# Attention scores accumulated over a whole head in four PSUM banks, four matmuls to one weight load

## The chip, the cores and the metric

The kernel runs on one core of a Trainium2 chip. The metric is the device time of one execution in microseconds (us), lower is better; the time given for a kernel is the median of several executions.

## The reference

One decode step of a transformer layer: layer norm, attention of one query token over a cache of 65,536 keys and values, then a gated MLP.

```python
q = (layernorm(x) @ wq)                  # 32 query heads of 128
# 8 KV heads, 4 query heads share one: k_cache, v_cache are [8, 65536, 128] bf16
scores = einsum("bhqd,bhkd->bhqk", q, k) * 128 ** -0.5
o = softmax(scores) @ v                  # per head
h = x + o @ wo
out = h + (sigmoid(g) * u) @ w_down      # g, u = layernorm(h) @ w_gate, @ w_up
```

K and V together are 268 MB, read once. Everything else is small.

## The kernel before

A KV head's 65,536 keys are four *blocks* of 4 MB (one DMA each), and a block is eight *chunks*. A ring of four 4 MB slots takes K and V blocks in turn; all loads are issued from one queue in a fixed order, each as soon as the load that had its slot is used up. DVE transposes each chunk of K in 32x32 pieces from the ring into a small key buffer; PE multiplies it with the query (which sits as "weights" in the array) and accumulates in a PSUM bank.

```python
NKT = 6          # key buffers, one chunk each
NS = 5           # PSUM banks for scores, one block each
...
def freed(ld):   # what a slot's next load waits for
    return {"wq": "q", "K": f"T{b}.{NC - 1}", "V": f"PV{b}"}[k]
...
def dve_block(b):
    for c in range(NC):                       # 8 chunks
        deps = [f"K{b}"] if c == 0 else []
        if n >= NKT: deps.append(f"S{(n - NKT) // NC}.{(n - NKT) % NC}")
        op("dve", lambda e, d=dst, sr=src: e.transpose(d, sr), deps, f"T{b}.{c}")
    op("dve", lambda e: e.tensor_reduce(M_sb[...], ps(b % NS, 0, 512), AX.X, ALU.max), [f"S{b}"], f"mx{b}")

def pe_scores(b):
    for c in range(NC):
        for je in range(4):                   # the weights differ for every (c, je)
            op("pe", lambda e, ...: e.matmul(ps(b % NS, 0, 512), lhsT=w_ap(h, je, c), rhs=kt_ap(n, je),
                start=(c == 0 and je == 0), stop=(c == NC - 1 and je == 3)), ...)
...
for b in range(NB + 4):                       # program order on every engine
    if b < NB:
        dve_block(b); pe_scores(b)
        if b % NR == NR - 1: softmax(b // NR)
    v = b - NR
    if v >= 0:
        if v % NR == 0: denominators(v // NR)
        pv(v)                                 # 32 matmuls, each with its own weights
        if v % NR == NR - 1: head_out(v // NR)
        if v == NB - 4: project7()
# ... last projection and the MLP follow
```

The weights of chunk c are the head's queries shifted by c columns, so that the eight chunks of a block land in different rows of one bank. That is why a block needs 32 weight loads for 32 matmuls.

## Time and profile before

| | before |
|---|---|
| time, median of 3 (range) | 667.71 us (667.36 to 667.81) |
| span of the profiled execution | 665.9 us |
| bytes read from HBM | 282.33 MB |
| DMA busy / PE / DVE / weight loads | 98.9% / 60% / 54% / 24% |

The first extract is from the page of the profile. Its first line gives busy time, share of the span and number of instructions; in the DMA strip each digit is a fortieth of the span in tenths; `q1` are the kernel's loads and `q8` instruction fetches (packets, MB, share of all DMA engines' time); the line that starts with DMA 67% is the chain of waits by engine; the last four are groups of instructions: busy us, mean ns | idle time of the engine before them and what ended it.

```profile
PE 396.3 (60%) x2545; PEld 162.8 (24%) x2545; DVE 359.2 (54%) x408; ACT 34.1 (5%) x90; POOL 8.5 (1%) x12
...
DMA  9999999999999999999999999999999999999996
...
q1 hardware_dynamic: 11560, 282.33, 98.9%
q8 instruction: 20, 0.33, 0.2%
...
DMA 67%; DVE 22%; PE 9%; ACT 1%; issue 0%; SPq 0%
...
L356 PE MATMUL PS<-ktw 128*128 128x512 bf16 x1024 | 294.1, 449 | 201.3 <-DVE ktw L342 196.1
L342 DVE STREAM_TRANSPOSE ktw<-ring 128x1024 f32<-128x1024 f32 x256 | 292.1, 1207 | 180.9 <-DMA ring<-in_A_k_cache_dram 180.9
L356 PEld LDWEIGHTS PS<-ktw 128*128 128x128 bf16 x1024 | 107.4, 110 | 384.6 <-DVE ktw L342 243.7
...
L343 DVE TENSOR_REDUCE M_sb<-PS 128x1 f32<-128x512 f32 x32 | 22.1, 692 | 49.9 <-PE PS L356 49.9
```

The DMA strip is full in all slices but the last, at a rate (282.33 MB over 665.9 us, 424 GB/s) near what the loads ever reach. The Trainium skill, "DMA: Bandwidth & Descriptors", section "Where 436 GB/s comes from", gives 435 GB/s as the ceiling of the path; the trace agrees with 431 to 432 in the steady state. PE idles 201 us before its score matmuls, nearly always for DVE, and DVE idles 181 us for K to land. So PE waits for DVE and DVE waits for DMA.

The second is from the chain of waits in order of time: start us, us, what.

```profile
57.08 1.05 PE PS L356 x4
...
121.26 9.14 DVE ktw L342 x8
...
130.42 29.67 DMA ring<-in_A_k_cache_dram
...
160.11 9.14 DVE ktw L342 x8
...
633.59 24.59 DMA ring<-in_B_w_up_dram
```

Two K/V pairs (16.78 MB) pass in 160.11 - 121.26 = 38.85 us, which is 432 GB/s. The 9.14 us of DVE in each period look like critical time, because a K load is issued when the transposes two K blocks earlier are done. But the load then takes 29.67 us to land, where 4.19 MB alone need 9.7: other loads are still ahead of it in the queue. Note also the first line, `57.08 1.05`: from the end of a block's last transpose to the end of its last four matmuls.

### The profile page before, as it was taken

What the parts mean: (1) busy time and instruction counts of PE and PEld (TensorE: products, weight loads), DVE (VectorE), ACT (ScalarE), POOL (GpSimd) and SP (SyncE); (2) the same over time, 40 slices, a digit from 0 to 9 for tenths busy, and PEclk for the clock granted to TensorE, in tenths of its full rate; (3) what the DMA queues carried; (4) which work ended last, traced back from release to release, by engine and by line L of the source; (5) the groups of instructions that cost most, each with busy time, mean ns of one, the idle gap of its engine ahead of it and who ended that gap; (6) DMA issues with size and microseconds to landing.
All of it is one profiled execution on the core that took longest, in us unless ns stands there. A gap on an engine that the chain in (4) does not pass through costs nothing.

```text
span 665.9 us, 5728 instructions
## 1 busy us (share of the span) xinstructions
PE 396.3 (60%) x2545; PEld 162.8 (24%) x2545; DVE 359.2 (54%) x408; ACT 34.1 (5%) x90; POOL 8.5 (1%) x12
## 2 busy tenths in 40 slices
PE   3778586565458664555665644666554567655344
PEld 2522232222123221222222212222221222223212
DVE  6579865574447655464555744476544645553002
ACT  0200100020002000020000200010000200002000
POOL 4000000000000000000000000000000000000000
PEclk9789798677787866788876778887677987768566
DMA  9999999999999999999999999999999999999996
GB/s 378 440 433 417 439 436 425 428 439 428 423 440 433 423 435 433 430 427 438 429 427 436 430 430 429 432 433 429 435 425 436 429 426 439 430 429 409 427 426 249
DMA packets 11586, 282.70 MB, mean 425 GB/s; under 512 B 1193, under 2 KB 2218, under 8 KB 2602
## 3 DMA queue, kind: packets, MB, share of 16 engines
q1 hardware_dynamic: 11560, 282.33, 98.9%
q8 instruction: 20, 0.33, 0.2%
q14 instruction: 4, 0.03, 0.0%
q10 hardware_dynamic: 2, 0.00, 0.0%
HBM read 282.33 MB, written 0.00 MB: 424 GB/s over the span
## 4 chain that ended last, share of the span: by engine, by line
DMA 67%; DVE 22%; PE 9%; ACT 1%; issue 0%; SPq 0%
DMA ring<-in_A_k_cache_dram 58%; DVE ktw L342 21%; PE PS L356 6%; DMA ring<-in_A_v_cache_dram 4%; DMA ring<-in_B_w_up_dram 4%; DMA ring<-in_A_wq_dram 2%; PE PS L307 1%; PE PS L419 1%; DVE M_sb L343 1%; ACT ktw L324 0%; DVE PT_sb L388 0%; PE PS L521 0%; PE PS L497 0%; SPq L239 0%; DVE hh L513 0%
## 5 line engine op out<-in xcount | busy, mean ns | idle before, releaser
L356 PE MATMUL PS<-ktw 128*128 128x512 bf16 x1024 | 294.1, 449 | 201.3 <-DVE ktw L342 196.1
L342 DVE STREAM_TRANSPOSE ktw<-ring 128x1024 f32<-128x1024 f32 x256 | 292.1, 1207 | 180.9 <-DMA ring<-in_A_k_cache_dram 180.9
L356 PEld LDWEIGHTS PS<-ktw 128*128 128x128 bf16 x1024 | 107.4, 110 | 384.6 <-DVE ktw L342 243.7
L419 PE MATMUL PS<-ring,PT_sb 128*16 128x512 bf16 x1024 | 70.6, 424 | 21.1 <-DMA ring<-in_A_v_cache_dram 21.1
L343 DVE TENSOR_REDUCE M_sb<-PS 128x1 f32<-128x512 f32 x32 | 22.1, 692 | 49.9 <-PE PS L356 49.9
L419 PEld LDWEIGHTS PS<-ring,PT_sb 128*16 128x16 bf16 x1024 | 28.4, 113 | 53.8 <-DMA ring<-in_A_v_cache_dram 25.3
L376 ACT ACTIVATE negmax<-PS 128x1 f32<-128x1 f32 x8 | 1.4, 171 | 550.2 <-PE PS L374 550.2
L388 DVE STREAM_TRANSPOSE PT_sb<-P_sb 128x512 bf16<-128x512 bf16 x32 | 21.8, 711 | 11.9 <-ACT P_sb L385 11.9
L433 DVE CAST O<-PS 128x4 bf16<-128x4 f32 x8 | 1.3, 162 | 39.1 <-PE PS L430 39.1
L385 ACT ACTIVATE P_sb<-PS,negmax 128x512 bf16<-128x512 f32 x32 | 21.6, 685 | 0.3
L307 PE MATMUL PS<-ring,xz 128*32 128x128 bf16 x128 | 9.7, 253 | 3.0 <-DMA ring<-in_A_wq_dram 3.0
L307 PEld LDWEIGHTS PS<-ring,xz 128*32 128x32 bf16 x128 | 9.6, 116 | 3.0 <-issue 3.0
L284 POOL TENSOR_TENSOR rstd<-ve,nhalf 128x1 f32<-128x1 f32 x2 | 1.1, 554 | 645.6 <-DVE ve L282 645.6
L430 PE MATMUL PS<-sel_bf,po_sb 128*128 128x4 bf16 x32 | 2.0, 168 | 11.4 <-ACT po_sb L427 11.4
L427 ACT ACTIVATE po_sb<-PS,rl 128x512 bf16<-128x512 f32 x8 | 5.5, 693 | 45.1 <-PE PS L419 45.1
L367 PE MATMUL PS<-identf,gm 128*1 128x128 f32 x16 | 3.0, 271 | 7.8 <-DVE gm L365 7.8
L385 ACT ACTIVATION_READ_ACCUMULATOR P_sb<-PS,negmax 128x1 f32 x32 | 6.5, 202 | 0.0
L456 PE MATMUL PS<-O,ktw 128*128 128x1 bf16 x128 | 4.9, 173 | 2.6 <-DMA ktw<-in_A_wo_dram 2.4
L257 DVE TENSOR_SCALAR rows_i<-rows_i 128x128 int32<-128x128 int32 x1 | 6.1, 6101 | 0.0
L259 DVE TENSOR_SCALAR cols_i<-cols_i 128x128 int32<-128x128 int32 x1 | 6.0, 6028 | 0.0
L374 PE MATMUL PS<-one_f,gmrep 1*128 1x1 f32 x16 | 3.0, 256 | 4.9 <-DVE gmrep L371 4.9
L456 PEld LDWEIGHTS PS<-O,ktw 128*128 128x128 bf16 x128 | 4.6, 118 | 2.9 <-DMA ktw<-in_A_wo_dram 2.2
(72 smaller groups left out, 56.8 us busy)
## 6 DMA issues: line engine op xcount, KB each, us to landing
ring<-in_A_k_cache_dram SPq DMA_DIRECT2D x32, 4096.0 KB, 29.7
ring<-in_A_v_cache_dram SPq DMA_DIRECT2D x31, 4096.0 KB, 35.6
ring<-in_A_wq_dram SPq DMA_DIRECT2D x1, 4096.0 KB, 12.1
ring<-in_A_v_cache_dram SPq DMA_DIRECT2D x1, 3072.0 KB, 32.6
ktw<-in_A_wo_dram SPq DMA_DIRECT2D x1, 2048.0 KB, 14.7
ktw<-in_A_wo_dram SPq DMA_DIRECT2D x2, 1024.0 KB, 18.1
ring<-in_B_w_gate_dram SPq DMA_DIRECT2D x1, 1792.0 KB, 38.5
ring<-in_B_w_up_dram SPq DMA_DIRECT2D x1, 1792.0 KB, 24.6
```

The source lines that it names most:

```text
L257: op("dve", lambda e: e.tensor_scalar(rows_i[:, :], rows_i[:, :], 3, 3, op0=ALU.arith_shift_right, op1=ALU.bitwise_and), ["rows"], "rows2")
L259: op("dve", lambda e: e.tensor_scalar(cols_i[:, :], cols_i[:, :], 3, None, op0=ALU.bitwise_and), ["cols"], "cols2")
L307: op("pe", lambda e, kt=kt, n=n, last=last: e.matmul(ps(1, 0, 128, 0, 32), lhsT=xz[:, kt * 63 + 31 - n: kt * 63 + 63 - n], rhs=wq_v[:, kt, ...
L342: op("dve", lambda e, d=dst, sr=src: e.transpose(d, sr), deps, f"T{b}.{c}")
L343: op("dve", lambda e: e.tensor_reduce(M_sb[:, b % 8:b % 8 + 1], ps(b % NS, 0, 512), AX.X, ALU.max), [f"S{b}"], f"mx{b}")
L356: op("pe", lambda e, n=n, je=je, c=c: e.matmul(ps(b % NS, 0, 512), lhsT=w_ap(h, je, c), rhs=kt_ap(n, je), start=(c == 0 and je == 0), stop ...
L367: op("pe", lambda e: e.matmul(ps(MISC, 0, 128, 0, 1), lhsT=gm[:, k:k + 1], rhs=identf[:, :], start=True, stop=True), [f"gm{h}", "identf", ...
L385: op("act", lambda e, b=b: e.activation(P_sb[:, (b % 4) * 512:(b % 4 + 1) * 512], ps(b % NS, 0, 512), AF.Exp, bias=negmax[:, k:k + 1], sca ...
L388: op("dve", lambda e, b=b: e.transpose(PT_sb[:, (b % 8) * 512:(b % 8 + 1) * 512], P_sb[:, (b % 4) * 512:(b % 4 + 1) * 512]), [f"E{b}", f"P ...
L419: op("pe", lambda e, lhsT=lhsT, tq=tq, t0=t0, c=c: e.matmul(ps(bank, 0, 512, 32 * tq, 32 * tq + 16), lhsT=lhsT, rhs=ring[:, s * SLOT + t0 ...
L427: op("act", lambda e: e.activation(po_sb[:, :], ps(PO_BANKS[k], 0, 512), AF.Copy, scale=rl[:, k:k + 1]), [f"PV{NR * h + NR - 1}", f"rl{h}" ...
L456: op("pe", lambda e, lhsT=lhsT, r=r, nt=nt, end=end: e.matmul(ps(YT, nt, nt + 1), lhsT=lhsT, rhs=src[:, r:r + 1], start=False, stop=end, s ...
```

## The change

Intent: save weight loads. A head now holds four PSUM banks over all its 32 chunks; chunk c of a block goes to bank c mod 4, so that four chunks in a row use the same shifted weights. Per half block and `je`, the first of four matmuls loads weights and the other three keep them (`ldweights=False`). The maxima can only be taken at the head's end, all four there. Two more key buffers (8 in place of 6) are paid for by letting an index table share memory with the probability buffers.

```diff
-NKT = 6
+NKT = 8
...
-            op("dve", lambda e: e.tensor_reduce(M_sb[:, b % 8:b % 8 + 1], ps(b % NS, 0, 512), AX.X, ALU.max),
-               [f"S{b}"], f"mx{b}")
+            if b % NR == NR - 1:
+                for k in range(NR):
+                    u = b - NR + 1 + k
+                    op("dve", lambda e, u=u: e.tensor_reduce(M_sb[:, u % 8:u % 8 + 1], ps(u % NS, 0, 512), AX.X, ALU.max),
+                       [f"S{b}.{NC - NR + k}"], f"mx{u}")
...
+        def matmul_kept(e, kept, out, lhsT, rhs, start, stop):
+            if not kept:
+                return e.matmul(out, lhsT=lhsT, rhs=rhs, start=start, stop=stop)
+            return e.add_instruction(mybir.InstMatmult(..., ldweights=False))
...
-            for c in range(NC):
-                ...
-                for je in range(4):
-                    op("pe", ... e.matmul(ps(b % NS, 0, 512), lhsT=w_ap(h, je, c), rhs=kt_ap(n, je), ...
+            for half in range(NC // NR):
+                for je in range(4):
+                    for k in range(NR):
+                        c = half * NR + k
+                        u = NR * h + k
+                        ...   # je == 0 waits for T{b}.{c}; a head's first also for E, mx of u - NS
+                        op("pe", ... matmul_kept(e, k > 0, ps(u % NS, 0, 512),
+                            w_ap(h, je, r * (NC // NR) + half), kt_ap(n, je), ...
# cut: the softmax's and PV's indices and waits follow the new layout; E_all is built in two pieces
```

## The prediction

> **What bounds the kernel.** The profile page gives a span of 665.9 us in which the 16 DMA engines are busy 98.9% and read 282.33 MB; the forty-slice strip has DMA at 9 in every slice but the last, while PE is at 60%, DVE 54%, weight loads 24%. The Trainium skill, "DMA: Bandwidth & Descriptors", section "Where 436 GB/s comes from", puts the fabric ceiling at 435 GB/s; the trace agrees: in the chain of waits two K/V pairs (16.78 MB) pass every 38.84 us, 432 GB/s. 282.33 MB at that rate is 653.5 us; start and tail are the rest. No change off the DMA can win more than a few us.
>
> The chain also charges 22% to DVE (key transposes) and 6% to score matmuls. I read this as not limiting: a K load is issued when the transposes two K blocks earlier end, but takes 29.7 us to land, and a 4.19 MB load alone needs 9.7 us. So about 20 us of other loads are outstanding at its issue; a later transpose shortens that queue, but doesn't empty it.
>
> **What the change does.**
> - Drops 768 of 1024 score weight loads, 110 ns each in the groups: PEld busy 163 -> about 80 us. Four matmuls of a chunk take 1.05 us in the chain, 263 ns each; the startup-free floor I estimate near 213 ns (512 columns at full clock), so up to 50 ns on 768, at most 38 us of PE time. PE already waits 196 us for transposes (waits view), so idle time is moved.
> - DVE keeps 256 transposes (1207 ns) and 32 maxima (692 ns). The maxima move to a head's end: three more there (2.1 us), but one stall for PE per head, not per block. DVE idle before maxima falls from 49.9 to about 20-25 us and becomes waiting for K (180.9 -> about 205-215).
> - A block's last transpose is followed by 13 matmuls (about 3 us), not 4 (1.05 us). At a head's end scores, maxima and softmax end about 4 us later; the next head's first transposes, idle 2 us before it now (timeline), start about 2 us late.
> - A head's first scores wait for the previous head's exponentials (0.7 us each). Eight key buffers let DVE run a block ahead.
> - Start: block 1's transposes no longer wait for block 0's maximum (DVE idle 4.7 us there), so head 0 ends some us earlier.
>
> **On the critical path.** Steady state: nothing; 2-4 us fit in 20 us of outstanding loads. Start: from 27 to 95 us the chain is PE and DVE, but loads stay outstanding (windows there show 418-462 GB/s), so the gain only deepens the queue. Tail: the output weights are issued when the last scores end (599.8 us), with a V load outstanding until 608.5 us; 2 us later fits. Then come V landing, PV (3.6 us), w_up landing (24.6 us) and 7.7 us of MLP, all unchanged.
>
> **Prediction.** 667.4 us against 667.71; range 665.5 to 669.5. Faster by over 2%: 1%; within 2%: 98%; slower by over 2%: 1%.
>
> **What would show it.** DMA share about 99%, 430 GB/s between 100 and 640 us as now (windows); K hops in the chain still 38.8 us per two pairs; 768 fewer weight loads; DVE waiting longer for K; scores ending about 3 us after a block's last transpose; MLP tail unchanged. PE busy may hardly fall: the granted clock (0.5 to 1.0 in the windows) weighs more than weight loads.
>
> **What would make it wrong.** A queue that empties at head starts (a window's DMA share well under 1); a DMA rate that changes with engine activity; a last head so late that output weights or last V blocks leave a gap near 600-615 us; matmuls with kept weights slower than DVE's pace.

## The result and the profile after

| | before | after |
|---|---|---|
| time, median of 4 (range) | 667.54 us (667.23 to 667.81) | 666.04 us (665.95 to 666.21) |
| span of the profiled execution | 665.9 us | 664.3 us |
| PE busy / weight loads busy | 396.3 / 162.8 us | 417.5 / 83.7 us |
| rate between 100 and 560 us | 431 GB/s | 431 GB/s |
| PE instruction fetches (`q8`) | 20 | 17 |

The outputs are right. The ratio is 0.9979 (95% interval 0.9965 to 0.9993), not quite the ratio of the medians. The same within 2%, as predicted, but a small real gain: about 1.5 us, which the prediction had only as -0.3. From the page of the changed kernel:

```profile
PE 417.5 (63%) x2545; PEld 83.7 (13%) x1777; DVE 357.3 (54%) x409; ACT 34.4 (5%) x90; POOL 8.5 (1%) x12
...
DMA  9999999999999999999999999999999999999996
...
q1 hardware_dynamic: 11560, 282.33, 99.1%
q8 instruction: 17, 0.28, 0.2%
...
DMA 71%; DVE 21%; PE 5%; SPq 2%; issue 0%; ACT 0%
...
L344 DVE STREAM_TRANSPOSE ktw<-ring 128x1024 f32<-128x1024 f32 x256 | 292.0, 1207 | 181.5 <-DMA ring<-in_A_k_cache_dram 181.1
L355 PE MATMUL PS<-ktw 128*128 128x512 bf16 x768 | 271.0, 451 | 53.6 <-DVE ktw L344 53.6
L354 PE MATMUL PS<-ktw 128*128 128x512 bf16 x256 | 118.5, 463 | 123.2 <-DVE ktw L344 123.2
...
L354 PEld LDWEIGHTS PS<-ktw 128*128 128x128 bf16 x256 | 27.5, 107 | 437.8 <-issue 275.3
...
L348 DVE TENSOR_REDUCE M_sb<-PS 128x1 f32<-128x512 f32 x32 | 19.9, 683 | 25.1 <-PE PS L354 25.1
...
L414 DVE TENSOR_REDUCE lsum<-PS 128x1 f32<-128x4 f32 x8 | 1.3, 161 | 27.7 <-PE PS L412 27.7
```

The DMA strip and share answer to those of before. The weight loads fell by 79 us, and PE did not get faster: its busy time rose. DVE's idle time before the maxima (L348) halved, from 49.9 to 25.1 us, but its idle time for K (L344) is what it was; the difference stands on the last line: 27.7 us before `lsum`, a reduction that waits for a small PE matmul queued behind the next head's first scores. Before, that wait came to 0.5 us in all (view of lines by form):

```profile
L396 DVE TENSOR_REDUCE lsum<-PS 128x1 f32<-128x4 f32 x8 | 1.2, 153 | 0.5 <-PE PS L394 0.5
```

From the chain of waits of the changed kernel, in order of time:

```profile
62.71 0.22 PE PS L354
62.93 0.65 PE PS L355 x3
...
79.63 0.43 PE PS L354
80.05 1.28 PE PS L355 x3
...
121.52 9.14 DVE ktw L344 x8
...
130.68 29.68 DMA ring<-in_A_k_cache_dram
...
160.38 9.14 DVE ktw L344 x8
...
642.48 18.15 DMA ring<-in_B_w_down_dram
```

Three things are to be seen. First, a matmul that loads its weights (L354) takes 0.22 us in the chain and three that keep them (L355) 0.65, so 0.217 each: no difference. At half clock (79.63) it is 0.43 against 1.28 for three, again none. Second, the steady state is 160.38 - 121.52 = 38.86 us per two pairs, as before. Third, the tail: the chain now ends over w_down, not w_up, because w_up lands at 657.0 us, 1.2 us before the 658.2 us at which it landed before (`633.59 24.59`). The V load ahead of it is 1 us earlier as well (628.85 against 629.89 us). So nearly the whole gain is in when the last loads land. The score matmuls, whose weight loads were saved, got no faster. The landings after the change, from its timeline (start us, us, what [idle before and what ended it]):

```profile
628.89 3.18 PE L438 MATMUL PS<-ring,PT_sb 128*16 128x512 bf16 x32 [8.42 <-DMA ring<-in_A_v_cache_dram]
...
656.99 0.93 PE L516 MATMUL PS<-ring,hc 128*1 128x448 bf16 x16 [1.57 <-DMA ring<-in_B_w_up_dram]
```

The trace's start times say the same of all score matmuls. Before, 662 of 1023 start-to-start distances lie between 200 and 300 ns with median 217, and 284 between 400 and 450 with median 427. After, the medians are 218 and 427 for the matmuls with a load, 217 and 427 for those without. The Trainium skill, "TensorE: Matmul & The Clock Gate", section "Step-by-step: what each phase is for", says that PE pulls a weight load ahead of the matmuls in flight; the trace agrees: the loads were hidden already.

### Where the landings differ

Each load's packets are spread over 16 DMA engines, and each engine closes its part of a load with a 4-byte write that the trace records (16 such writes to a load; the records do not name the engine). Sorting these writes by load gives, for every load, how far each engine lags behind the foremost one (worked out from the trace's DMA records, not a view of the profile). For the V block of head 7 that is issued just before the output weights, in us (a bar marks a gap in the row):

```
before  foremost lands 602.70 us after the first packet; lags:
  0.00 0.05 0.12 0.15 0.22 0.28 0.87 | 3.06 3.09 3.19 3.25 3.31 3.39 3.41 3.47 3.57
after   foremost lands 602.69;  lags:
  0.00 0.10 0.19 0.19 0.22 0.40 0.76 | 1.66 1.80 2.01 3.08 3.27 3.31 3.46 3.47 3.85
```

The foremost engines keep time to 0.01 us in the two kernels at this load. About half of the engines fall behind in steps over the run, each time one 16 KB packet of `q8` passes, and a load is complete only when its last engine is. Nine engines stand behind here, not eight: the 8 KB packets of `q14`, another instruction queue, set back engines too, by some 0.5 to 1 us each, and one of the nine has been set back only by those.

The gain is not there yet at this load: its last engine is 3.57 us behind before the change and 3.85 after. It shows at the V load ahead of `w_up`. By then 18 fetches have passed before the change and 15 after it:

```
before  foremost lands 623.23 us; lags:
  0.00 0.04 0.20 0.34 0.35 0.49 0.53 | 2.51 2.63 2.69 2.77 2.86 2.94 3.05 | 4.14 4.40
after   foremost lands 622.75;  lags:
  0.00 0.09 0.18 0.18 0.22 0.37 0.72 1.62 | 3.10 3.30 3.31 3.34 3.50 3.50 3.61 3.89
```

Two engines stand out before the change, as many as the fetches beyond sixteen. Of the 1.0 us by which this load lands earlier, 0.51 us is the lag of the last engine; the foremost engine is 0.48 us earlier as well, and what moved it was not settled. e2_pad_784 and e9_pad_280 below are closer pairs for the fetches alone. The Trainium skill, "Runtime: NRT & Kernel Launch", section "Instruction fetch mechanics", says that an engine's instructions are streamed in blocks of 16 KiB, 256 instructions, over a DMA queue that the sequencer drives itself. This agrees with the count: 2545 matmuls and 2545 weight loads are 5090 PE instructions, or 19.9 blocks (20 packets); after, 2545 + 1777 = 4322, or 16.9 (17 packets). The durations of these packets repeat with period eight in the trace, so they seem to go to eight of the sixteen engines in turn.

That gave **theory A**: the gain is three instruction fetches fewer; each costs one DMA engine some time, and the engine that has had most of them sets the end. **Rival B**: the gain comes from the new order and buffers. **Rival C**: matmuls with kept weights are faster after all.

### The profile page after: what moved, and what is told of

Read it like the earlier page. It is cut to its first block, busy times and chain, and to the rows that moved or that the text cites. A ratio compares the mean times of both kernels' runs of the same rounds, so it can differ in the third digit from the quotient of the medians.

```text
span 664.3 us, 4982 instructions
## 1 busy us (share of the span) xinstructions
PE 417.5 (63%) x2545; PEld 83.7 (13%) x1777; DVE 357.3 (54%) x409; ACT 34.4 (5%) x90; POOL 8.5 (1%) x12
## 3 DMA queue, kind: packets, MB, share of 16 engines
q1 hardware_dynamic: 11560, 282.33, 99.1%
## 4 chain that ended last, share of the span: by engine, by line
DMA 71%; DVE 21%; PE 5%; SPq 2%; issue 0%; ACT 0%
DMA ring<-in_A_k_cache_dram 62%; DVE ktw L344 20%; DMA ring<-in_A_v_cache_dram 4%; DMA ring<-in_B_w_down_dram 3%; PE PS L355 2%; DMA ring<-in_A_wq_dram 2%; SPq L230 1%; PE PS L309 1%; PE PS L354 1%; PE PS L438 1%; DVE PT_sb L406 0%; DVE M_sb L348 0%; SPq L239 0%; PE PS L540 0%; ACT P_sb L403 0%
## 5 line engine op out<-in xcount | busy, mean ns | idle before, releaser
L344 DVE STREAM_TRANSPOSE ktw<-ring 128x1024 f32<-128x1024 f32 x256 | 292.0, 1207 | 181.5 <-DMA ring<-in_A_k_cache_dram 181.1
L355 PE MATMUL PS<-ktw 128*128 128x512 bf16 x768 | 271.0, 451 | 53.6 <-DVE ktw L344 53.6
L354 PE MATMUL PS<-ktw 128*128 128x512 bf16 x256 | 118.5, 463 | 123.2 <-DVE ktw L344 123.2
L438 PE MATMUL PS<-ring,PT_sb 128*16 128x512 bf16 x1024 | 74.9, 444 | 18.8 <-DMA ring<-in_A_v_cache_dram 18.8
L354 PEld LDWEIGHTS PS<-ktw 128*128 128x128 bf16 x256 | 27.5, 107 | 437.8 <-issue 275.3
L348 DVE TENSOR_REDUCE M_sb<-PS 128x1 f32<-128x512 f32 x32 | 19.9, 683 | 25.1 <-PE PS L354 25.1
L414 DVE TENSOR_REDUCE lsum<-PS 128x1 f32<-128x4 f32 x8 | 1.3, 161 | 27.7 <-PE PS L412 27.7
L385 PE MATMUL PS<-identf,gm 128*1 128x128 f32 x16 | 3.4, 298 | 16.9 <-DVE gm L383 16.9
## 6 DMA issues: line engine op xcount, KB each, us to landing
ring<-in_A_k_cache_dram SPq DMA_DIRECT2D x32, 4096.0 KB, 29.7
```

The lines of the kernel that those rows point to most:

```text
L348: op("dve", lambda e, u=u: e.tensor_reduce(M_sb[:, u % 8:u % 8 + 1], ps(u % NS, 0, 512), AX.X, ALU.max), [f"S{b}.{NC - NR + k}"], f"mx{u}")
L354: return e.matmul(out, lhsT=lhsT, rhs=rhs, start=start, stop=stop)
L355: return e.add_instruction(mybir.InstMatmult(name=nc.get_next_instruction_name(), engine=mybir.EngineType.PE, ins=[e.lower_ap(rhs), e.lowe ...
L438: op("pe", lambda e, lhsT=lhsT, tq=tq, t0=t0, c=c: e.matmul(ps(bank, 0, 512, 32 * tq, 32 * tq + 16), lhsT=lhsT, rhs=ring[:, s * SLOT + t0 ...
```

## The experiments

The kernel before ran beside each call: 667.33 us (e1 to e4), 667.39 us (e5 to e7) and 667.43 us (e8, e9). The three calls ran on three different chips, and the changed kernel was not run again in them; so runs of different calls are compared by way of the kernel before, which stays within 0.21 us over all four calls.

### e1_all_loads: the new order with all weight loads back

```diff
-                        ... matmul_kept(e, k > 0, ps(u % NS, 0, 512), ...
+                        ... matmul_kept(e, False, ps(u % NS, 0, 512), ...
```

> The changed kernel with its order, banks and 8 key buffers, but with every score matmul loading its weights again (768 loads back). Theory A (the small gain comes from PE's instruction stream: one 16 KB fetch per 256 instructions occupies one of the DMA engines that bring K and V, and the engine with most fetches sets the end): fetches back from 17 to 20, time back to 667.0 to 667.9 us. Rival B (the gain comes from the new order and buffers): time stays at 666.0 +- 0.3. Both: matmul spacing stays at 217 ns at full clock and 427 ns at half clock, PE busy within 2% of the changed kernel's 417.5 us, because a load is hidden behind the matmul before it. Rival C (kept weights make matmuls faster): PE busy or spacing rises.

Measured: 667.41 us (667.26 to 667.49), ratio 1.0000. From its page:

```profile
PE 420.6 (63%) x2545; PEld 165.6 (25%) x2545; DVE 357.4 (54%) x409; ACT 34.4 (5%) x90; POOL 8.5 (1%) x12
...
q8 instruction: 20, 0.33, 0.2%
```

With 20 fetches the time is back at the kernel before, so new order, banks and buffers by themselves bring nothing: B falls. PE busy is 420.6 us against 417.5 with kept weights, and the spacings are 217 and 427 ns: C falls too. It also shows that the rise of PE busy from 396.3 us belongs to the new order, not to keeping weights; why the order does that was not pursued.

### e2_pad_784: the changed kernel with idle instructions in place of the loads

```diff
                 if v == NB - 4:
                     project7()
+            if NR <= b < NB:     # two such waits become one instruction
+                op("pe", lambda e: [e.wait_ge(P.dma_sems["x"]["sem"], 16) for _ in range(56)][-1])
```

> The changed kernel unchanged in work, plus 784 PE instructions that do nothing (waits on a semaphore long satisfied, 28 at the end of each of 28 blocks, where PE idles). Theory A: 3 more fetches (20), time 666.6 to 667.9. Rival B: 666.0 +- 0.3.

Measured: 667.33 us (667.07 to 667.73), ratio 1.0000, 20 fetches. The gain vanishes though PE's work is that of the changed kernel. So it is the number of instructions, not what they do. At the V load ahead of `w_up` the foremost engine is within 0.11 us of the changed kernel's, and the last one is 1.3 us later:

```
e2_pad_784  foremost lands 622.86 us; lags:
  0.00 0.21 0.22 0.25 0.32 0.34 0.92 | 3.03 3.06 3.38 3.41 3.41 3.59 3.77 | 4.74 5.09
```

### e3_pad_2044: the kernel before with idle instructions

The same edit in the kernel before, with `range(146)`.

> The kernel before plus 2044 PE instructions that do nothing (73 at the end of each of 28 blocks). Theory A: 8 more fetches; the fetch durations repeat with period 8 in the trace, so each of 8 DMA engines gets exactly one more, whatever the phase: +0.5 to +0.9 us, to 668.0 to 668.5. Rival B: 667.5 +- 0.2.

Measured: 669.02 us (668.72 to 669.21), ratio 1.0024 (1.0011 to 1.0037). From its page:

```profile
q8 instruction: 27, 0.44, 0.3%
```

The direction is A's, the size is about twice what I expected: +1.7 us for 7 fetches more. I had put a fetch at 0.6 us, 16 KB at a sixteenth of 432 GB/s. The lags at the same V block show the true size:

```
e3_pad_2044  foremost lands 602.67 us; lags:
  0.00 0.05 0.07 0.08 0.14 0.35 0.73 | 3.15 4.76 4.76 4.76 4.81 4.87 4.89 4.89 4.95
```

24 fetches have passed by then, and eight engines stand at 4.76 to 4.95. Two fetches had set an engine back to about 3.1 to 3.5 us, three set it back to 4.8: about 1.5 us each. The foremost engine is where it was, so the waits on PE did not starve the queue.

### e4_quarter_scores: a quarter of the score matmuls (wrong on purpose)

```diff
-                for je in range(4):
+                for je in range(1):
```

(in `pe_scores` of the kernel before, with `stop` and the names moved to `je == 0`)

> Wrong result on purpose: the kernel before with one score matmul per chunk in place of four (768 matmuls and 768 loads gone, PE busy down by about 200 us). If PE or its weight loads were on the critical path in the steady state, the time falls by far more than 2 us, towards 650. DMA bound with theory A: 14 fetches, time between 665.3 and 667.2, K landings still 38.8 us per two pairs.

Measured: 666.03 us (665.92 to 666.14), ratio 0.9980. From its page:

```profile
PE 300.4 (45%) x1777; PEld 89.1 (13%) x1777; DVE 359.2 (54%) x408; ACT 34.7 (5%) x90; POOL 8.4 (1%) x12
...
q8 instruction: 14, 0.23, 0.1%
```

PE busy fell by 96 us (not the 200 I had written: at the lower clock, 0.57, what is left takes longer), and the time by 1.3 us, to that of the changed kernel within 0.01 us. So neither score matmuls nor their weight loads bound anything in the steady state. 14 and 17 fetches cost the same: both are at most two turns of eight engines, as the seventeenth passes only when the data are through (trace times 671.94 against 671.92 us).

### e5_late8 and e6_late28: how late may a head start?

```diff
+                if b % NR == 0 and b and c == 0:
+                    for i in range(7):       # 24 in e6_late28
+                        op("dve", lambda e, d=dst, sr=src: e.transpose(d, sr), deps, f"X{b}.{i}")
+                        deps = [f"X{b}.{i}"]
                 op("dve", lambda e, d=dst, sr=src: e.transpose(d, sr), deps, f"T{b}.{c}")
```

(in the changed kernel)

> The changed kernel with the first transpose of every head but the first made 7 times more (each waits for the one before; same source and target, result right): DVE is about 8.3 us later at each of 7 head starts, so a K load is issued that much later. Theory (about 20 us of other loads are outstanding when a K load is issued, so a late head start costs nothing): 666.0 +- 0.5, DMA at 430 GB/s between 100 and 560 us. Rival (the chain's 20% of DVE is time on the critical path): +8.3 x 7 = up to 58 us longer.

> The same with 24 extra transposes, about 28.5 us later at 7 head starts. If the cover is 18 to 20 us, the queue runs dry for about 8 to 12 us at each: 666 + 50 to 100 us, with windows of low GB/s at head starts. If the cover is much larger, less; if it is much smaller, the 8 us run is slower too.

Measured: e5_late8 668.31 us (668.11 to 668.39), 2.3 us over the changed kernel; e6_late28 783.82 us (782.90 to 784.49), 118 us over it. Windows of e5_late8 (stretch: length, busy of PE, weight loads, DVE, ACT and POOL, granted clock, DMA share, GB/s), then of e6_late28:

```profile
90.00:92.00 2.00, 2.00 (x11) 0.19 (x2) 0.56 (x1) 0.00 (x0) 0.00 (x0) 1.00 0.86 246
92.00:94.00 2.00, 2.00 (x11) 0.19 (x2) 0.00 (x0) 0.00 (x0) 0.00 (x0) 1.00 0.75 311
...
100.00:560.00 460.00, 286.53 (x1593) 48.37 (x1019) 304.67 (x316) 21.77 (x60) 0.00 (x0) 0.76 1.00 431
```

```profile
92.00:116.00 24.00, 9.97 (x30) 0.91 (x8) 19.95 (x17) 0.00 (x0) 0.00 (x0) 0.56 0.13 44
116.00:200.00 84.00, 37.20 (x240) 7.28 (x163) 65.93 (x65) 3.64 (x10) 0.00 (x0) 0.71 0.90 387
200.00:217.00 17.00, 13.89 (x74) 2.29 (x44) 13.34 (x14) 0.00 (x0) 0.00 (x0) 0.80 0.59 236
```

In e5_late8 the seven repeats take 8.9 us. The queue ran thin just once, at the first head start (246 and 311 GB/s between 90 and 94 us), and never after: 431 GB/s from 100 to 560 us. The foremost engine's landings agree: +2.4 us at the first K load after that, and no further loss at the six later head starts. So the chain's 20% of DVE is not time on the critical path at those head starts, and the rival of +58 us falls; that a faster DVE would win nothing was not tested by itself. In e6_late28 the repeats take 30.6 us at the first head start, and the foremost engine's landings slip by 24.2 us at the first head start and by 15 to 17 us at each of the next three looked at. The cover is the difference: about 6 us at the first head start (8.9 - 2.4 = 6.5 in the one kernel, 30.6 - 24.2 = 6.4 in the other), and about 14 us later. The prediction's 20 us were too many. It took the 29.7 us that the slowest engine needs to land a load, and the foremost engines run dry 2 to 4 us earlier, by their lags; what makes up the rest was not settled. The change's own delay at the last head's end, 2.3 us, is below either.

### e7_pad_4088: twice as many idle instructions

The edit of e3_pad_2044 with `range(292)`.

> The kernel before plus 4088 PE instructions that do nothing (146 at the end of each of 28 blocks): 16 more fetches than before, two full turns of the 8 DMA engines. From the lags in the trace (each fetch sets one engine back about 1.5 us) and from the run with 2044 (+1.7 us): +3.0 to +3.6 us, 670.3 to 671.0. If the run with 2044 was slow for another reason (PE late), the growth is not linear and the least delayed DMA engine also falls back.

Measured: 866.22 us (864.69 to 868.70). This run says nothing on fetches. The longest waits (in total us, times, longest us):

```profile
PE PS L356 <- issue: 393.1, 27, 15.8
```

In the trace the 146 instructions of a block take 15.7 to 16.0 us and start 106 ns apart (median), and PE then had no time left in its 19.4 us per block (half of the 38.86 us for two pairs). In e3_pad_2044 the 73 take 7.7 to 8.2 us and still fit. My expectation had named this way to fail, but not that it was near.

### e8_quarter_both: under one turn of fetches (wrong on purpose)

The edit of e4_quarter_scores, and in `pv`:

```diff
-                for tq in range(4):
+                for tq in range(1):
```

> Wrong result on purpose: the kernel before with one score matmul per chunk in place of four and one PV matmul per chunk in place of four, 1536 matmuls and their loads gone; about 8 fetches, at most one per DMA engine before the data ends. Fetch theory (each turn of the 8 engines costs about 1.5 us: 8 to 16 fetches 666.0, 17 to 24 fetches 667.4, 27 669.0): 664.0 to 665.2 us. Rival (fewer fetches cannot win below the changed kernel; 666.0 is the DMA floor): 665.7 to 666.2.

Measured: 665.53 us (665.39 to 665.95), ratio 0.9972, 8 fetches. Between my two expectations: below the supposed floor of 666.0, but with a third of the step that I had forecast. The lags offer a reason, in the one execution that was traced: at the same V block nine engines stand at 0.00 to 0.64 us, six at 1.12 to 2.33, and a single one at 3.31. That one went from 2.3 to 3.3 us as an 8 KB packet of `q14`, another instruction queue, passed at 467 us in the trace. One such engine would be enough to hold the end; no run here takes that packet away to show it.

### e9_pad_280: the changed kernel at the edge of the third turn

The edit of e2_pad_784 with `range(20)`.

> The changed kernel plus 280 PE instructions that do nothing (10 at the end of each of 28 blocks): one or two fetches more (18 or 19), so the third turn has just begun on one or two engines. Staircase theory (the most burdened engine sets the end): most of the step is there already, 666.7 to 667.6. Rival (a cost proportional to fetches, 0.45 us each): 666.4 to 666.9. Rival B (schedule): 666.0 +- 0.3.

Measured: 667.25 us (666.68 to 667.64), 18 fetches, ratio 0.9995 to the kernel before. One fetch more than the changed kernel, the first of the third turn to pass before the data are through, and the median is 1.2 us higher: most of the step, as the staircase has it. The trace shows the place. The V load ahead of `w_up` lands no later than in the changed kernel (its last engine at 626.24 us after the first packet against 626.64), and `w_up` is issued at the same time (632.17 against 632.12 us). Then the seventeenth fetch passes, at 649.6 us, and `w_up` lands at 658.0 us in place of 657.0:

```profile
632.17 25.84 DMA ring<-in_B_w_up_dram
```

The runs of this kernel scatter more than the others', and the lowest would fit the proportional rival; against that, 14 and 17 fetches give 666.03 and 666.04 us.

### All together

| kernel | PE instruction fetches | time, us |
|---|---|---|
| e8_quarter_both (wrong) | 8 | 665.53 |
| e4_quarter_scores (wrong) | 14 | 666.03 |
| changed kernel | 17 | 666.04 |
| e9_pad_280 | 18 | 667.25 |
| before | 20 | 667.33 to 667.54 |
| e1_all_loads, e2_pad_784 | 20 | 667.41, 667.33 |
| e3_pad_2044 | 27 | 669.02 |

Kernels with quite different PE work fall in the order of this number alone, in steps rather than on a straight line. e5_late8, e6_late28 and e7_pad_4088 are left out, as other things hold them.

## Why the prediction was right, and where it was not

**Right: DMA bounds the kernel, and the change leaves it the same.** 666.04 us lies in the range 665.5 to 669.5. That the range holds it is owed to its width of 4 us: the prediction had no term for most of the 1.5 us. DMA share 99.1%, 431 GB/s, 38.86 us per two pairs: all as said. e4_quarter_scores shows it beyond the change: with three quarters of the score matmuls gone, the time moves by 1.3 us.

**Right: weight loads busy fall to about 80 us** (83.7), scores end later after the last transpose at a head's end (the output weights are issued at 602.1 us in place of 599.8, 2.3 us later against "2 us later"), and head 0's softmax starts earlier (67.2 against 69.8 us).

**Wrong in size: "up to 50 ns on 768, at most 38 us of PE time".** The term is zero. The 1.05 us for four matmuls, from which I took 263 ns each and set them against an assumed floor, hold the end of the last matmul as well as four distances of 217 ns; a chain entry that starts with a wait and ends with a result is no measure of spacing. Start times were in the trace and would have shown 217 ns at once. e1_all_loads confirms it.

**Wrong in size: "about 20 us of other loads are outstanding".** About 14 us, and about 6 at the first head start, by e5_late8 and e6_late28. It did no harm, as the delay is 2 to 4 us.

**Wrong in place: DVE's idle time "becomes waiting for K (180.9 -> about 205-215)".** It stayed at 181.1. The 25 us that left the maxima came back before `lsum` (27.7 us): an instruction in DVE's order that waits for a PE matmul, and PE's score bursts now end later.

**Missing: the instruction stream as load on the DMA engines.** The prediction counted bytes of data, and had no term for 768 instructions of 64 bytes, 3 of 20 blocks. They are 0.02% of the bytes, but each block sets back one of sixteen engines by about 1.5 us, and the last engine decides. The fetches account for the gain of 1.5 us to within the noise of these runs: restoring the count restores the time, with the weight loads (e1_all_loads) or without them (e2_pad_784).

What stays open: why a 16 KB fetch costs its engine about 1.5 us when its own packet is recorded with about 1.07 us, and which of the sixteen engines carry the fetches; that there are eight is inferred from lags and from the period of the durations. Why the foremost engine is 0.48 us earlier at the V load ahead of `w_up` is open too. No kernel here is faster than the changed one with a right result. The next step down would need PE to have under about nine blocks, 2300 instructions, and the scores and PV alone take 1280 and 2048.

## What to carry to other kernels

Before saving weight loads, look at the start-to-start distance of the matmuls: if it is the same with a load and without one (here 217 or 218 ns at full clock, 427 at half), the loads are hidden and nothing is to be had on PE. In a kernel that is bound by DMA, an engine's share of the chain of waits is not a cost until the queue behind it runs dry; delay that engine on purpose to see how far off that is. And when such a kernel shifts by a fraction of a per cent for no visible reason, compare the instruction counts: fetches travel on the same DMA engines as the data.

## What the Trainium skill lacked or had wrong

- "Runtime: NRT & Kernel Launch", section "Instruction fetch mechanics", calls the cost of crossing a 16 KiB boundary "mostly hidden". Whether PE itself waits at a fetch was not looked at. For this kernel, bound by DMA, the cost is not hidden: a fetch set one DMA engine back by about 1.5 us, and 17, 20 and 27 fetches gave 666.04, 667.33 to 667.54 and 669.02 us. The page lacks that the fetches seem to use eight of the sixteen engines in turn, so that the cost comes in steps (14 and 17 fetches: 666.03 and 666.04 us; 18: 667.25 us).
- "TensorE: Matmul & The Clock Gate", section "Back-to-back issue gap", gives about 131 ns per matmul of 512 columns for a sustained stream of load and matmul pairs. Here the medians were 217 to 218 ns at full and 427 ns at half clock, with a load before each matmul or before every fourth; the section's formula for a gap, an estimate of 216 and 427 ns for 512 columns, fits, the 131 ns do not.
- "DMA: Bandwidth & Descriptors", section "Where 436 GB/s comes from", says without a condition that for transfers between HBM and SBUF the limit of about 358 GB/s binds; the note just above that section ties this figure to both cores of a pair streaming. This kernel, on one core, read at 431 GB/s for 460 us, near the 435 of the same section.
- No page that I found gives the cost on PE of a wait for a semaphore that is already satisfied: in e7_pad_4088 such instructions started 106 ns apart (median).
